# Balanced routing on one NeuronCore: each expert's list built inside its own round, and a token's state kept as one number in place of a one-hot row

## The chip, the core and the metric

The kernel runs on one core of a Trainium2 chip. The metric is device time in microseconds (us), from the timed runs of the whole program; a profiled execution, taken separately, shows what each engine does. The engines are TensorE (PE, with its weight loads listed as PEld), VectorE (DVE), ScalarE (ACT), GpSimd (POOL) and SyncE (SP, which here only issues DMAs).

## The reference, cut to what matters

Two blocks follow each other. The first is a gated linear attention with a state of 48 x 48 per head, over 4 sequences of 768 steps and 8 heads. Its output, as a matrix x of 3072 tokens by 384, goes into a layer of 8 experts with a fixed capacity:

```python
cap = N // E                                  # 3072 / 8 = 384 tokens for each expert
logits = x @ w_gate
order = np.argsort(-logits.flatten())         # all (token, expert) pairs, best first
for idx in order:
    tok, e = (int(idx) // E, int(idx) % E)
    if assigned[tok] >= 0 or counts[e] >= cap:
        continue
    assigned[tok] = e
    counts[e] += 1
for e in range(E):
    mask = assigned == e
    out[mask] = np.maximum(x[mask] @ w1[e], 0.0) @ w2[e]     # 384 -> 1024 -> 384
```

So every token gets one expert and every expert exactly 384 tokens. The greedy order matters only where an expert fills up: until then each token simply takes its best open expert.

## The kernel before, in words

**Attention** runs to about 170 us and ends with `logits`, a tile of 128 partitions by 24 columns by 8 experts: a token is one partition and one column. Alongside it, `begin` and its inner `part` prepare round 0: each token's best expert as a one-hot row `choice`, and `over`, how far its best logit lies above a lower bound.

**Rounds.** `assign_and_run` replaces the greedy loop by seven rounds and a rest. A round (loop at L825) closes one expert at least. It finds, for the tokens without an expert, their best open expert (`choices`, L521), then searches for the level at which the first expert has as many takers as places (`search`, L587), and assigns every token above that level (`assign`, L608). The level is found digit by digit, five digits of 15 steps each. For one digit DVE compares `over` with 15 steps for all 24 columns (`above`, 128 x 360), PE counts takers per step and expert (`cnt`), and DVE picks the digit. Round 0 uses `digit_alone` (L539), with 24 small count matmuls and one that spreads the digit (L550). Later rounds use `digit_beside` (L554), with three count matmuls (L560) and one that sums over partitions (L575). `close` (L654) then sets the state for the next round.

**State.** `assigned` is a one-hot row of 8 per token. `choices` reduces it to `taken`, 0 or 1, to leave assigned tokens out. `left` numbers the experts that have no list yet, from 1 to 8.

**Lists.** `expert_list` (L660) returns twelve steps that make the list of one filled expert. `members` picks the expert `m`, its one-hot row `sel`, and by a product with `assigned` (`mine`) and a reduction the tokens of it (`member`). `place` counts along the columns and lets PE sum over the partitions before (`before`, L682). `index` reads the expert's number into SP and issues the DMAs of its weights. `lines` turns a token's place into one of three blocks of 128 lines (`pl`, `b`, `line`), while POOL prepares `number` (L711 to L715). Six steps `in_line` (L719) compare lines with 1 to 128, four columns of 128 at a time, into a 0/1 matrix of 128 x 24 x 128. `used` strikes the expert off. `tokens` (L732) multiplies that matrix by the tokens' numbers in 24 matmuls (L735), turns the sums into token numbers, lets POOL gather the rows of x by indirect DMA (L745), and puts the expert's work in a queue.

**The order of the work** is written out by hand, for PE, DVE, ACT and POOL. Two queues hold what is not yet issued. `pe_work` holds the pieces of the experts' work: for an expert three turns (three transposes each, L772), 24 pieces of the first product (`up`, L783) and 24 of the second (`down`, L794), 51 pieces in all. `dve_work` holds the steps of a list. `some(queue, n)` issues the next n. A digit of `digit_beside` issues `slots[0]` pieces ahead of its L560 and `slots[1]` ahead of L575, and one and two list steps behind these. The slots are 2 and 1 in rounds 1 and 2, and 4 and 3 from round 3 on; the first digit of rounds 2 and 3 has 4 more. `assign` issues two pieces ahead of its matmul `sums` (L617) and eight behind. When a list is done and at least 12 pieces are queued, the last two of them are moved behind the new expert's turns.

The lists of rounds 0, 1 and 2 are made at once, in the round that fills the expert: in round 0 beside `idle_turns` (L811), matmuls without use that keep PE busy, in rounds 1 and 2 with a piece of `pe_work` behind each step. From round 3 on the list stays in `dve_work` and is made during the next round's search. After the last round the tokens left over take the last open expert and its list is made. With nothing else to come, the remaining pieces run to the end.

There is a second way through, `exact`, which runs only if the decays were out of range or the search did not end well. It is not run here.

The steps above act through a few helpers, so most DVE rows of the profile carry a helper's line: L396 is `tt` (two tensors), L400 `ts` (a tensor and one or two scalars), L403 `stt` (tensor, scalar, tensor), L406 `reduce`. A scalar is a constant or one value per partition.

Of the kernel before, what the change touches and what calls it, by code (L numbers as in the profile page):

```python
# [2 lines left out]

# [7 lines left out]
FP32 = mybir.dt.float32  # L11
# [13 lines left out]
def kernel(  # L25
# [313 lines left out]

    first = ramp(E, "first", -1, E + 1)  # L340
# [67 lines left out]

    places = rt([E], "places", FP32, 1)
# [4 lines left out]
    assigned = rt([NT, E], "assigned", BF16, 1)  # L414
# [52 lines left out]
    def begin():  # L467

        nc.vector.memset(places[:], float(CAP))
        nc.vector.memset(wanted[:], float(CAP))  # L470
        nc.vector.memset(penalty[:], 0.0)
        nc.vector.memset(full[:], 1.0)
        nc.vector.tensor_copy(out=left[:], in_=count[:, 0:E])
        nc.vector.memset(assigned[:], 0.0)
        nc.vector.memset(lowest[:], 0.0)
        choice, over = rt([NT, E], "choice", BF16), rt([NT], "over")

        def part(c0, c1):
            n = c1 - c0

            def of(t):
                return t[:].rearrange("p (b c) -> p b c", b=B)[:, :, c0:c1]

            def of_e(t):
                return t[:].rearrange("p (b c) e -> p b c e", b=B)[:, :, c0:c1]

            def over_e(t):
                return t.unsqueeze(3).to_broadcast((128, B, n, E))

            best, pick = rt([B, n], "best0"), rt([B, n], "pick0")  # L490
# [6 lines left out]
            reduce(pick[:], masked[:], ALU.max)  # L497
            tt(of_e(choice), masked[:], over_e(pick[:]), ALU.is_equal)

        return (choice, over), part  # L500

    def assign_and_run(begun=None, also=None, again=None, exact=None):
# [18 lines left out]
        def choices():  # L521
# [8 lines left out]
            reduce(pick[:], masked[:], ALU.max)  # L530

            taken = rt([NT], "taken")
            reduce(taken[:], assigned[:], ALU.max)
            stt(pick[:], taken[:], 100.0, pick[:], ALU.mult, ALU.add)
            choice = rt([NT, E], "choice", BF16)
            tt(choice[:], masked[:], col(pick[:], E), ALU.is_equal)
            return choice, best

        def digit_alone(above, choice, unit):  # L539

            r = bank("cnt", "r")
            for c in range(NT):
                nc.tensor.matmul(out=r[0:NTH, 0:E], lhsT=above[:, c, :], rhs=choice[:, c, :],
                                 start=(c == 0), stop=(c == NT - 1))
# [42 lines left out]
        def search(choice, over, digits, slots, first=0):  # L587

            digit = None
            for steps, unit, size in digits:  # L590
                above = rt([NT, NTH], "above", BF16)
                if digit is None:
                    tt(above[:], col(over[:], NTH), row(steps[:], NTH), ALU.is_ge)
                else:
                    stt(above[:], col(over[:], NTH), digit, row(steps[:], NTH), op, ALU.is_ge)
                    new = rt([NT], "over")
                    ts(new[:], over[:], digit, op)
                    over = new
                if slots:
                    digit, op = digit_beside(above, choice, size, (slots[0] + first, slots[1]))  # L600
                else:
                    digit, op = digit_alone(above, choice, unit)
                first = 0
            new = rt([NT], "over")
            ts(new[:], over[:], digit, op)
            return new

        def assign(choice, over, slots):  # L608
# [10 lines left out]
            tt(assigned[:], assigned[:], sure[:], ALU.add)  # L619
# [3 lines left out]
        def assign_exact(choice, over, slots):  # L623
# [17 lines left out]
            tt(assigned[:], assigned[:], sure[:], ALU.add)  # L641
# [10 lines left out]
            tt(assigned[:], assigned[:], tie[:], ALU.add)  # L652
# [7 lines left out]
        def expert_list():  # L660
# [3 lines left out]
            def members():  # L664
                score, m, sel = rt([E], "score"), rt([1], "m"), rt([E], "sel")
# [33 lines left out]
            def lines():  # L699
# [3 lines left out]
                tt(pl[:], L["incl"][:], L["r"][:, 0:1].to_broadcast((128, NT)), ALU.add)  # L703
                tt(pl[:], pl[:], L["member"][:], ALU.mult)
# [14 lines left out]
            def in_line(c0, c1):  # L719
                def go():  # L720
                    n = c1 - c0
                    tt(L["in_line"][:, c0:c1],
                       L["line"][:, c0:c1].unsqueeze(2).to_broadcast((128, n, 128)),
                       count[:].unsqueeze(1).to_broadcast((128, n, 128)), ALU.is_equal)
                return go

            def used():
                used = rt([E], "used")
                stt(used[:], left[:], 1.0, L["sel"][:], ALU.add, ALU.mult)
                tt(left[:], left[:], used[:], ALU.subtract)  # L730

            def tokens():  # L732
                r = bank("tokens", "r")
                for c in range(NT):
                    nc.tensor.matmul(out=r[:, 0:2 * TE], lhsT=L["in_line"][:, c, :],  # L735
                                     rhs=L["number"][:, c].rearrange("p a n -> p (a n)"),
                                     start=(c == 0), stop=(c == NT - 1))
                pair = rt([2, TE], "pair")
# [19 lines left out]
                in_line(c, c + PART) for c in range(0, NT, PART)] + [used, tokens]  # L758
# [59 lines left out]
        with tc.manual_schedule(engines=engines):  # L818
# [5 lines left out]
            beside_choices = {2: 4, 3: 4}  # L824
            for rnd in range(E - 1):  # L825
                slots, more = pace.get(rnd, (4, 3)), beside_choices.get(rnd, 0)
                if exact:
                    choice, best = choices()
# [9 lines left out]
                else:  # L838
                    if rnd == 0:
                        choice, over = begun  # L840
                    else:
                        choice, best = choices()
                        over = rt([NT], "over")
                        level_keys(best[:], over[:])
# [21 lines left out]
            while dve_work:  # L866
                some(dve_work, 1)
                some(pe_work, 1)
            choice, _ = choices()
            tt(assigned[:], assigned[:], choice[:], ALU.add)  # L870
# [148 lines left out]
```

## Time and profile before

| | us |
|---|---|
| median of three timed runs | 509.3 (509.28 to 511.03) |
| the profiled execution's own time | 511.35 |
| its span, first to last instruction | 509.6 |
| PE busy | 459.8 (90%) |
| DVE busy | 268.6 (53%) |
| ACT busy | 128.4 (25%) |
| POOL busy | 110.3 (22%) |
| mean granted PE clock | 0.964 |
| first piece of the first product (L783) starts | 201.0 |
| last PE instruction ends | 499.9 |

How to read it: busy time is that of executed instructions; a matmul's end is modelled and holds its drain, so rows of PE overlap a little. In a timeline a row gives the start, the duration (for several merged instructions, from the first start to the last end), the engine, line and operation, what is written from what, the shapes and a count; in brackets stands the idle time of the engine ahead of it and what ended that. The row PEclk shows the clock granted to PE in 40 slices of the span, in tenths.

### The profile page before, as it was taken

What the parts mean: (1) busy time and instruction counts of PE and PEld (TensorE: products, weight loads), DVE (VectorE), ACT (ScalarE), POOL (GpSimd) and SP (SyncE); (2) the same over time, 40 slices, a digit from 0 to 9 for tenths busy, and PEclk for the clock granted to TensorE, in tenths of its full rate; (3) what the DMA queues carried; (4) which work ended last, traced back from release to release, by engine and by line L of the source; (5) the groups of instructions that cost most, each with busy time, mean ns of one, the idle gap of its engine ahead of it and who ended that gap; (6) DMA issues with size and microseconds to landing.
All of it is one profiled execution on the core that took longest, in us unless ns stands there. A gap on an engine that the chain in (4) does not pass through costs nothing.

```text
span 509.6 us, 11773 instructions
## 1 busy us (share of the span) xinstructions
PE 459.8 (90%) x4848; PEld 304.0 (60%) x4848; DVE 268.6 (53%) x887; ACT 128.4 (25%) x301; POOL 110.3 (22%) x172
## 2 busy tenths in 40 slices
PE   2999999999999579898899998699899989999992
PEld 1778888887888435455466555355556555656551
DVE  6466666666677474766754568168666671000000
ACT  2455455544432001111111210121120210212210
POOL 2134333333231012013022003101303233002010
PEclk9999999999999659999999999599999999999997
DMA  9988997985211034053072007107243576000000
GB/s 158 187 167 178 192 201 165 188 172 123 66 34 50 17 130 165 1 207 117 17 251 74 16 13 283 47 6 258 78 163 124 184 237 239 32 0 33 14 17 35
DMA packets 118399, 59.11 MB, mean 116 GB/s; under 512 B 101664, under 2 KB 112960, under 8 KB 118336
## 3 DMA queue, kind: packets, MB, share of 16 engines
q1 hardware_dynamic: 111760, 44.06, 34.9%
q0 software_dynamic: 3072, 9.44, 5.7%
q10 hardware_dynamic: 3504, 4.77, 2.7%
q8 instruction: 40, 0.66, 0.6%
q14 instruction: 23, 0.19, 0.1%
HBM read 48.77 MB, written 9.49 MB: 114 GB/s over the span
## 4 chain that ended last, share of the span: by engine, by line
PE 63%; issue 17%; DVE 11%; POOL 4%; DMA 2%; ACT 1%; POOLq 0%; DVEq 0%
PE H L783 15%; PE O L794 14%; PE Y L247 5%; PE T L193 4%; PE A L230 4%; PE L L161 4%; PE L L165 3%; PE Y L257 2%; PE X L273 2%; PE dS L212 2%; DMA xe<-xd,token 2%; POOL out_dram L799 2%; PE X L287 2%; POOL xe L745 2%; DVE above L403 2%
## 5 line engine op out<-in xcount | busy, mean ns | idle before, releaser
L783 PE MATMUL H<-xeT,w 128*128 128x384 f32 x384 | 134.5, 499 | 1.7 <-ACT xeT L775 1.7
L794 PE MATMUL O<-w,hT 128*128 128x384 f32 x384 | 132.3, 492 | 0.5 <-issue 0.5
L783 PEld LDWEIGHTS H<-xeT,w 128*128 128x128 f32 x384 | 70.9, 193 | 52.8 <-issue 8.8
L794 PEld LDWEIGHTS O<-w,hT 128*128 128x128 f32 x384 | 70.1, 190 | 46.7 <-issue 5.6
L787 ACT ACTIVATE hT<-H 128x384 f32<-128x384 f32 x64 | 31.4, 491 | 114.2 <-PE H L783 111.2
L799 POOL DMA_INDIRECT out_dram<-o,token x24 | 24.3, 1014 | 143.7 <-ACT o L798 142.8
L235 DVE COPY_PREDICATED am<-mask,A 128x512 f32<-128x512 int32 x48 | 32.4, 727 | 29.0 <-PE A L230 29.0
L798 ACT COPY o<-O 128x384 f32<-128x384 f32 x24 | 11.5, 479 | 101.0 <-PE O L794 94.5
L396 DVE TENSOR_TENSOR in_line<-line,count 128x512 bf16<-128x512 f32 x48 | 31.6, 708 | 0.2
L745 POOL DMA_INDIRECT xe<-xd,token x24 | 24.1, 1004 | 34.1 <-DVE best L406 7.4
L185 POOL TENSOR_TENSOR kg<-k,ek 128x384 f32<-128x384 f32 x24 | 25.4, 1057 | 28.0 <-ACT ek L173 22.3
L161 PE MATMUL L<-g,wcum 128*128 128x384 f32 x48 | 23.0, 564 | 8.1 <-DVE count L329 8.1
L247 PE MATMUL Y<-v,am 128*64 128x48 f32 x768 | 28.0, 224 | 0.0
L247 PEld LDWEIGHTS Y<-v,am 128*64 128x64 f32 x768 | 24.7, 138 | 4.0 <-issue 3.7
L775 ACT COPY xeT<-Xe 128x384 f32<-128x384 f32 x24 | 10.6, 483 | 64.4 <-PE Xe L772 63.6
L230 PE MATMUL A<-qT,kT 48*64 48x128 f32 x768 | 26.7, 278 | 0.0
L711 POOL TENSOR_TENSOR past<-b,ramp_nt 128x48 f32<-128x48 f32 x8 | 2.2, 278 | 106.1 <-DVE b L396 106.1
L170 DVE TENSOR_SCALAR dl<-L 128x384 f32<-128x384 f32 x24 | 13.4, 557 | 21.1 <-PE L L165 21.1
L165 PEld LDWEIGHTS L<-ind,g 128*64 128x64 f32 x384 | 13.9, 144 | 14.1 <-issue 14.1
L396 DVE TENSOR_TENSOR own<-cnt,mine 120x64 f32<-120x64 f32 x30 | 6.7, 223 | 29.5 <-PE cnt L560 29.1
L230 PEld LDWEIGHTS A<-qT,kT 48*64 48x64 f32 x768 | 21.5, 137 | 0.2
L172 ACT ACTIVATE eq<-dl 128x384 f32<-128x384 f32 x24 | 12.6, 523 | 29.4 <-DVE dl L170 28.8
(170 smaller groups left out, 584.9 us busy)
## 6 DMA issues: line engine op xcount, KB each, us to landing
w<-in_moe_w_dram SPq DMA_DIRECT2D x16, 1536.0 KB, 8.6
f<-in_f_logit_dram SPq DMA_DIRECT2D x24, 192.0 KB, 4.7
q<-in_q_dram SPq DMA_DIRECT2D x24, 192.0 KB, 4.2
k<-in_k_dram SPq DMA_DIRECT2D x24, 192.0 KB, 4.6
v<-in_v_dram SPq DMA_DIRECT2D x24, 192.0 KB, 4.4
xd<-x ACTq DMA_DIRECT2D x24, 192.0 KB, 3.4
xe<-xd,token POOLq DMA_INDIRECT x24, 3.1
out_dram<-o,token POOLq DMA_INDIRECT x24, 2.6
```

Source lines behind the costliest of these rows:

```text
L161: nc.tensor.matmul(out=Lv, lhsT=wcum[:], rhs=g[:, :, 0:DH], start=True, stop=True)
L165: nc.tensor.matmul(out=ends[DP * r:DP * r + DP, :, hp], lhsT=g[:, 2 * hp + r, :], rhs=ind[:], start=True, stop=True)
L185: nc.gpsimd.tensor_tensor(out=kg[:, :, 0:DH], in0=G["k"][:], in1=ek[:], op=ALU.mult)
L230: nc.tensor.matmul(out=A[par][HC * j:HC * j + HC, 128 * hp:128 * hp + 128], lhsT=G["kT"][rows, hp, HC * j:HC * j + HC], rhs=G["qT"][rows, ...
L235: nc.vector.copy_predicated(am[:, par], mask[:].unsqueeze(1).to_broadcast((128, HP, 128)), A[par][:].rearrange("s (a t) -> s a t", t=128))
L247: nc.tensor.matmul(out=Y[par][HC * j:HC * j + HC, DH * hp:DH * hp + DH], lhsT=G["am"][:, par, hp, HC * j:HC * j + HC], rhs=G["v"][:, 2 * h ...
L396: nc.vector.tensor_tensor(out=out_, in0=a, in1=b, op=op)
L745: nc.gpsimd.indirect_dma_start(out=xe[:], out_offset=None, in_=xd[:, :], in_offset=bass.IndirectOffsetOnAxis(ap=token[:, i:i + 1], axis=0))
L783: nc.tensor.matmul(out=L["H"][:, 0:CAP], lhsT=L["w1"][:, d, 128 * ft:128 * ft + 128], rhs=xT[:, d, :], start=(d == 0), stop=(d == DC - 1))
L787: nc.scalar.activation(out=hT[:, ft, :], in_=L["H"][:, 0:CAP], func=AF.Relu)
L794: nc.tensor.matmul(out=L["O"][:, 0:D], lhsT=hT[:, ft, 128 * i:128 * i + 128], rhs=L["w2"][:, ft, :], start=(ft == 0), stop=(ft == FC - 1))
L799: nc.gpsimd.indirect_dma_start(out=outs[next(tiles)][:, :], out_offset=bass.IndirectOffsetOnAxis(ap=L["token"][:, i:i + 1], axis=0), in_=o ...
```

## The change

Four things change.

- **Every list at once.** The list is made in its own round in every round, with one piece of `pe_work` behind each of its twelve steps (in round 0 two idle turns behind each but the last two, so far three behind each). The slots from round 3 on become 3 and 2, the first digit of every round from 2 on gets 4 more, and `assign` has three pieces ahead of its matmul and seven behind. `used` goes behind `tokens`.
- **A number per token.** `taken` is no longer 0 or 1: it holds the number of the token's expert (8 for expert 0 down to 1), and 0 for a token without one. `assigned`, `mine` and `sel` go. `member` is one comparison of `taken` with `m`. `take` writes it, in two steps. `choices` keeps assigned tokens out by a large negative term in `over`. `left` runs from 8 to 1, so of several filled experts the lowest comes first, and the expert's number takes one more step.
- **Lines by column.** Each of the 24 columns is compared in an instruction of its own, with its line as the scalar, against a new bf16 tile `counts` of 1 to 128.
- **Round 0 in parts.** `above` is computed in three parts of eight columns, each ahead of the count matmuls that use it, and the step that brings `over` up to date goes behind the matmul that spreads the digit. The token sums of round 0's list are issued four columns at a time, behind their comparisons.

The diff, without the parts of the exact way:

```diff
@@ begin @@
-        nc.vector.tensor_copy(out=left[:], in_=count[:, 0:E])
-        nc.vector.memset(assigned[:], 0.0)
+        nc.vector.tensor_copy(out=left[:], in_=first[:])
+        nc.vector.memset(taken[:], 0.0)
...
-        def choices():
+        def picks():
...
-
-            taken = rt([NT], "taken")
-            reduce(taken[:], assigned[:], ALU.max)
-            stt(pick[:], taken[:], 100.0, pick[:], ALU.mult, ALU.add)
-            choice = rt([NT, E], "choice", BF16)
+            return best, pick, masked
+
+        def choices(best, pick, masked):
+
+            over, choice = rt([NT], "over"), rt([NT, E], "choice", BF16)
+            level_keys(best[:], over[:])
+            stt(over[:], taken[:], CLOSED / 16, over[:], ALU.mult, ALU.add)
             tt(choice[:], masked[:], col(pick[:], E), ALU.is_equal)
-            return choice, best
-
-        def digit_alone(above, choice, unit):
+            return choice, over
...
+        def take(over, pick, op=ALU.is_ge):
+            new = rt([NT], "new")
+            stt(new[:], over, 0.0, pick[:], op, ALU.mult)
+            tt(taken[:], taken[:], new[:], ALU.add)
+
+        def reached(above, over, digit, op, steps, c0, c1):
+
+            n = c1 - c0
+            over = over[:, c0:c1].unsqueeze(2).to_broadcast((128, n, NTH))
+            steps = steps[:].unsqueeze(1).to_broadcast((128, n, NTH))
+            if digit is None:
+                tt(above[:, c0:c1], over, steps, ALU.is_ge)
+            else:
+                stt(above[:, c0:c1], over, digit, steps, op, ALU.is_ge)
+
+        def digit_alone(above, parts, choice, unit):
 
             r = bank("cnt", "r")
             for c in range(NT):
+                if c % 8 == 0:
+                    parts(c, c + 8)
                 nc.tensor.matmul(out=r[0:NTH, 0:E], lhsT=above[:, c, :], rhs=choice[:, c, :],
                                  start=(c == 0), stop=(c == NT - 1))
...
@@ search, round 0 @@
-                    digit, op = digit_alone(above, choice, unit)
+                    new, op_new = digit_alone(above, parts, choice, unit)
+                    over = less(over, digit, op)
+                    digit, op = new, op_new
...
@@ assign @@
-            tt(assigned[:], assigned[:], sure[:], ALU.add)
+            take(over[:], pick)
...
@@ expert_list: members @@
-                ts(sel[:], left[:], m[:], ALU.is_equal)
-                mine = rt([NT, E], "mine", BF16)
-                tt(mine[:], assigned[:], row(sel[:], E), ALU.mult)
                 member = rt([NT], "member")
-                reduce(member[:], mine[:], ALU.max)
-                L.update(member=member, m=m, sel=sel)
+                ts(member[:], taken[:], m[:], ALU.is_equal)
+                L.update(member=member, m=m)
...
@@ index @@
-                ts(e[:], L["m"][:], -1.0, ALU.add, 0.0, ALU.max)
+                ts(e[:], L["m"][:], -1.0, ALU.mult, float(E), ALU.add)
+                ts(e[:], e[:], E - 1, ALU.min)
...
@@ lines @@
-                tt(pl[:], L["incl"][:], L["r"][:, 0:1].to_broadcast((128, NT)), ALU.add)
-                tt(pl[:], pl[:], L["member"][:], ALU.mult)
+                stt(pl[:], L["incl"][:], L["r"][:, 0:1], L["member"][:], ALU.add, ALU.mult)
...
@@ in_line @@
-                    n = c1 - c0
-                    tt(L["in_line"][:, c0:c1],
-                       L["line"][:, c0:c1].unsqueeze(2).to_broadcast((128, n, 128)),
-                       count[:].unsqueeze(1).to_broadcast((128, n, 128)), ALU.is_equal)
+                    for c in range(c0, c1):
+                        ts(L["in_line"][:, c], counts[:], L["line"][:, c:c + 1], ALU.is_equal)
+                    if alone:
+                        token_sums(c0, c1)
...
-                in_line(c, c + PART) for c in range(0, NT, PART)] + [used, tokens]
+                in_line(c, c + PART) for c in range(0, NT, PART)] + [tokens, used]
...
@@ the rounds @@
-            beside_choices = {2: 4, 3: 4}
             for rnd in range(E - 1):
-                slots, more = pace.get(rnd, (4, 3)), beside_choices.get(rnd, 0)
+                slots, more = pace.get(rnd, (3, 2)), 4 if rnd > 1 else 0
...
-                some(dve_work, len(dve_work))
-                (assign_exact if exact else assign)(choice, over, (2, 8))
-                dve_work.extend(expert_list())
+                (assign_exact if exact else assign)(choice, over, pick, (3, 7))
+                dve_work.extend(expert_list(rnd == 0))
+                while dve_work:
+                    some(dve_work, 1)
+                    if rnd:
+                        some(pe_work, 1)
+                    elif len(dve_work) > 1:
+                        idle_turns(2)
                 if rnd == 0:
-                    while dve_work:
-                        some(dve_work, 1)
-                        idle_turns(3)
                     idle_turns(27)
...
-                if rnd in (1, 2):
-                    while dve_work:
-                        some(dve_work, 1)
-                        some(pe_work, 1)
                 close()
...
-            choice, _ = choices()
-            tt(assigned[:], assigned[:], choice[:], ALU.add)
+            best, pick, masked = picks()
+            unassigned = rt([NT], "unassigned")
+            ts(unassigned[:], taken[:], -1.0, ALU.mult)
+            take(unassigned[:], pick)
```

More of the change, by code (lines that the diff above doesn't have):

```diff
@@ L413 @@
     left = rt([E], "left", FP32, 1)
[L414 removed]
+    taken = rt([NT], "taken", FP32, 1)
     lowest = rt([E], "lowest", FP32, 1)
@@ L496, in part @@
                first[:].unsqueeze(1).unsqueeze(1).to_broadcast((128, B, n, E)), ALU.mult)
-            reduce(pick[:], masked[:], ALU.max)
-            tt(of_e(choice), masked[:], over_e(pick[:]), ALU.is_equal)
-        return (choice, over), part
+            reduce(of(pick), masked[:], ALU.max)
+            tt(of_e(choice), masked[:], over_e(of(pick)), ALU.is_equal)
+        return (choice, over, pick), part
     def assign_and_run(begun=None, also=None, again=None, exact=None):
@@ L618, in assign, with assign_exact, take_all @@
             some(pe_work, slots[1])
-            tt(assigned[:], assigned[:], sure[:], ALU.add)
+            take(over[:], pick)
             tt(places[:], places[:], r[:, 0:E], ALU.subtract)
             ts(full[:], places[:], 0.5, ALU.is_lt)
-        def assign_exact(choice, over, slots):
+        def assign_exact(choice, over, pick, slots):
+            def take_all(mask):
+                some_ = rt([NT], "some")
+                reduce(some_[:], mask[:], ALU.max)
+                take(some_[:], pick, ALU.is_gt)
             after, notfirst, _ = exact
@@ L728, in used, with token_sums, tokens @@
                 used = rt([E], "used")
-                stt(used[:], left[:], 1.0, L["sel"][:], ALU.add, ALU.mult)
+                ts(used[:], left[:], L["m"][:], ALU.is_equal)
+                stt(used[:], left[:], 1.0, used[:], ALU.add, ALU.mult)
                 tt(left[:], left[:], used[:], ALU.subtract)
[L732 to L735, printed above, removed]
+            def token_sums(c0, c1):
+                if c0 == 0:
+                    L["sums"] = bank("tokens", "r")
+                for c in range(c0, c1):
+                    nc.tensor.matmul(out=L["sums"][:, 0:2 * TE], lhsT=L["in_line"][:, c, :],
                                      rhs=L["number"][:, c].rearrange("p a n -> p (a n)"),
                                      start=(c == 0), stop=(c == NT - 1))
+            def tokens():
+                if not alone:
+                    token_sums(0, NT)
+                r = L["sums"]
                 pair = rt([2, TE], "pair")
```

62 lines of the change are left out of this document (34 added, 28 removed).

## The prediction

> **What bounds the kernel now.** I read the page first, for the shape of the span, then busy time by stage, then the timeline of TensorE (PE) and VectorE (DVE) from the first choice to the last list, then who waited for whom.
>
> ```profile
> span 509.6 us, 11773 instructions
> ...
> PEclk9999999999999659999999999599999999999997
> ```
> ```profile
> 181.50:192.40 10.90, 9.48 (x61) 4.98 (x61) 7.33 (x25) 0.00 (x0) 1.30 (x3) 0.63 0.55 200
> 316.50:332.50 16.00, 10.13 (x51) 5.77 (x51) 4.70 (x21) 2.42 (x5) 3.76 (x4) 0.68 0.16 50
> ```
>
> A slice of the page is 12.7 us. The clock row drops twice after the attention part: in slices 14 and 15 (round 0) and in slice 26. The windows say the same (columns: stage, length, busy time of PE, its weight loads, DVE, ACT, POOL, then granted clock, DMA share, GB/s): from 316.5 to 332.5 the granted clock is 0.68 and PE is busy for 10.13 of 16 us. PE is the bound from 201 us on, since the experts' products are all there is left to do; what can be won there is only time in which PE stands still or runs at a low clock. These are the places:
>
> ```profile
> 316.51 0.21 PE L575 MATMUL cnt<-parts,ones 120*128 120x120 bf16 x1 [0.95 <-DVE parts L396]
> 316.57 0.75 PE L735 MATMUL tokens<-number,in_line 128*128 128x6 bf16 x24
> 321.12 0.90 PE L772 MATMUL Xe<-ident,xe 128*128 128x128 f32 x3 [3.81 <-DMA xe<-xd,token]
> ...
> 325.07 1.65 PE L783 MATMUL H<-xeT,w 128*128 128x384 f32 x2 [0.57 <-ACT xeT L775]
> ...
> 326.78 3.50 PE L783 MATMUL H<-xeT,w 128*128 128x384 f32 x6
> ...
> 332.49 0.17 PE L617 MATMUL sums<-count,ones 128*128 128x8 bf16 x1 [0.80 <-DVE count L406]
> ```
> ```profile
> 361.94 0.49 PE L772 MATMUL Xe<-ident,xe 128*128 128x128 f32 x3
> 362.27 0.22 PE L575 MATMUL cnt<-parts,ones 120*128 120x120 bf16 x1
> ...
> 365.34 8.01 PE L783 MATMUL H<-xeT,w 128*128 128x384 f32 x24 [0.54 <-ACT xeT L775]
> ```
> ```profile
> 415.57 0.16 PE L682 MATMUL before<-total,ltri 128*128 128x1 bf16 x1 [1.52 <-DVE e L400]
> ```
> ```profile
> PE sums L617 <- DVE count L406: 5.3, 6, 1.2
> ```
>
> What PE's queued work costs when nothing stops it:
>
> ```profile
> 223.80 0.17 PE L682 MATMUL before<-total,ltri 128*128 128x1 bf16 x1
> 223.83 6.70 PE L794 MATMUL O<-w,hT 128*128 128x384 f32 x20
> 230.36 0.75 PE L735 MATMUL tokens<-number,in_line 128*128 128x6 bf16 x24
> ```
>
> A product is two matmuls. 20 of them fill 223.83 to 230.36, so a queued product (a "piece") costs 0.653 us, and a "turn" of three transposes 0.33 (361.94 to 362.27). An expert is 3 turns and 48 products, 51 pieces. In round 4 the queue of pieces is empty when the tokens of the next expert are still being found: its list, put off into that round's search, has twelve steps, handed out three to a digit, so that the tokens come with the fourth.
>
> **The change, rounds 1 to 7.** The pieces are the same before and after, so I count only stalls. First those that go.
>
> (1) Round 4. From 316.5 to 332.5 PE has the token sums (0.75), nine transposes (1.0), six pieces (3.9: the rows with x2 and x6, and the two behind the last L575) and small things (0.2): 5.85 of 16 us. The six pieces show the low clock too, at 0.58 a matmul (3.50 by 6). Leave out the 0.8 at the end (next point but one), add the 0.95 ahead of 316.51, and 10.3 us are lost. In the new order a round hands out 5 digits of 3+2 pieces, 4 more in its first, 3+7 in the assignment and 12 beside its own list: 51, one expert. The queue, counted through: 49 pieces after round 0; round 1 takes 15 + 10 + 10 up to its tokens, which add 51, and 2 behind them: 63; round 2 the same with 4 more: 73; and then each round takes 29 + 10 + 10, which leaves 24 at the tokens, and ends at 73 again. Two of the 24 are set behind the turns, and so 22 pieces, 14.4 us, stand before the first transpose, which needs 4.6 (316.57 to 321.12). The stall goes, and the low clock with it. (2) Round 5: 361.94 to 365.34 is 3.4 us, with 1.1 of work: 2.3 go, for the same reason. (3) The `sums` matmul waits 0.8 us in five of these rounds (six waits of 5.3 in all, less round 0's 1.2). Three pieces before it in place of two fill 0.653 of that: 3.3 in all. (4) The last list: `before` waits 1.52. PE gets one piece more ahead of it (0.65), and DVE's chain from the tokens to `total` loses the wide steps `taken`, `choice`, `assigned`, `mine` and `member` and gains the narrow ones of `used`, `close` and `take`: some 0.6 shorter by their rows' sizes, between 0 and 0.9. I take 1.2 as gone. Sum: 17.1.
>
> Now what comes late instead. A digit needs time on DVE between its two matmuls:
>
> ```profile
> 212.42 0.21 PE L575 MATMUL cnt<-parts,ones 120*128 120x120 bf16 x1 [0.21 <-DVE parts L396]
> ...
> 214.22 0.35 PE L560 MATMUL cnt<-choice,above 128*120 128x64 bf16 x3 [0.24 <-DVE above L403]
> ...
> 215.51 0.21 PE L575 MATMUL cnt<-parts,ones 120*128 120x120 bf16 x1 [0.21 <-DVE parts L396]
> ```
>
> 1.80 us must pass from one digit's L575 to the next L560, and 1.29 from there to L575. Three pieces are 1.96, two are 1.31: PE hides both, barely, and a digit of rounds 3 to 6 becomes PE's 3.5 us. When turns fall into a digit (fourth digit of each round by my count), one piece and two turns are 1.31 against 1.80, one turn and one piece 0.98 against 1.29: 0.6 lost, four times, 2.4. Rounds 1 and 2 keep their 2+1 and lose what they lost. Net of rounds 1 to 7: 17.1 - 2.4 = 14.7 us.
>
> All this asks that the list itself stays hidden, now in every round:
>
> ```profile
> 224.04 0.18 DVE L396 TENSOR_TENSOR pl<-mincl,before 128x24 f32<-128x24 f32 x1 [3.64 <-PE before L682]
> ...
> 225.14 3.96 DVE L396 TENSOR_TENSOR in_line<-line,count 128x512 bf16<-128x512 f32 x6
> ```
> ```profile
> 141.65 0.25 DVE L400 TENSOR_SCALAR unit<-ones,step 128x128 bf16<-128x128 bf16 x1
> 141.81 0.23 DVE L400 TENSOR_SCALAR steps<-count,step 128x15 f32<-128x15 f32 x1
> 141.95 0.25 DVE L400 TENSOR_SCALAR unit<-ones,step 128x128 bf16<-128x128 bf16 x1
> ```
>
> `used` moves behind `tokens`, so 9 pieces, 5.88 us, lie between `before` and the tokens (10 so far). DVE needs 5.3 (223.80 to 229.10) so far. The new comparison is one instruction a column. Its nearest row is `unit`: same operation, 128 bf16 elements, a scalar per partition. It lasts 0.25, and the next starts 0.16 after it. 24 x 0.16 + 0.09 = 3.93: nothing is won on DVE, nothing lost, and with one step of `lines` less (0.21) the list needs 5.1, with 0.8 to spare. From below, a column costs the 0.14 of the step on 15 elements (141.81 to 141.95), 3.4 in all, a gain that PE's pieces would hide; from above there is no overlap at all, 24 x 0.246 = 5.9 (a rival). I take 0.16, the row of the same size. The Trainium skill says, in "VectorE: DVE Perf Modes", section "The DRAIN you can't avoid", that after every operation the pipe empties before the next starts, which speaks against cutting six instructions into 24. The trace does not agree for independent ones, by these rows; by the page's rule the time would be that rival's.
>
> **Round 0**, where PE has only idle turns to fill with.
>
> ```profile
> 172.22 0.60 DVE L403 SCALAR_TENSOR_TENSOR above<-over,cnt,steps 128x360 bf16<-128x360 f32 x1 [0.25 <-PE cnt L550]
> 172.73 0.24 DVE L400 TENSOR_SCALAR over<-over,cnt 128x24 f32<-128x24 f32 x1
> ...
> 172.87 0.75 PE L543 MATMUL cnt<-choice,above 128*15 128x8 bf16 x24 [0.69 <-DVE above L403]
> ```
> ```profile
> 181.59 1.12 PE L815 MATMUL nothing<-idle,ones 128*128 128x384 bf16 x3
> ...
> 182.83 0.36 DVE L396 TENSOR_TENSOR mine<-assigned,sel 128x192 bf16<-128x192 bf16 x1
> ...
> 183.61 0.21 DVE L677 TENSOR_TENSOR_SCAN mincl<-onesc,member 128x24 f32<-128x24 f32 x1
> ...
> 184.06 0.16 PE L682 MATMUL before<-total,ltri 128*128 128x1 bf16 x1 [1.36 <-DVE e L400]
> ...
> 184.98 0.28 POOL L711 TENSOR_TENSOR past<-b,ramp_nt 128x48 f32<-128x48 f32 x1 [26.13 <-DVE b L396]
> ...
> 185.75 0.62 POOL L715 TENSOR_TENSOR number<-past 128x144 bf16<-128x144 f32 x1
> ...
> 191.62 0.75 PE L735 MATMUL tokens<-number,in_line 128*128 128x6 bf16 x24
> ```
> ```profile
> DMA to landing us min/median/max: 3.0/3.1/5.2
> ```
>
> A digit: a third of `above` costs about 0.34 (between 0.24 for 24 elements and 0.60 for 360) and lets the next start after 0.25, so the thirds end at 0.34, 0.59 and 0.84; eight matmuls (0.25) behind the last end at 1.14 where all 24 now end at 1.40. 0.26 in four digits; the first waits for `choice` and wins nothing. The `over` step moves between `filled` and the next `above` and takes the gap there (0.24 in 0.25): I take 0.9. `sel` becomes `member`, `mine` and the old `member` go: 183.61 - 182.83 = 0.78. The two steps of `take` replace one under the wait for `sums`: 0, at most 0.2. `before` comes 1.7 earlier, at 182.4. Then PE sets the pace: 6 idle turns of 0.32 (1.12 for three, less the last one's drain; the clock is low here), then six groups of four token matmuls (0.13) with two idle turns (0.64) between: 5.9 us, sums done at 188.3; now they end at 192.37. DVE's columns are done at 187.4, so PE ends last. 4.1 us earlier. The second scalar step for the expert's number costs the weights' issue 0.1 and nothing behind it. One thing can take some back: the gathers now start while the first weights are still flying; a gather lands in 3.0 to 5.2, so up to 2.2 is lost. I take 4.0, bounds 1.8 and 4.7.
>
> **The sum.** 14.7 + 4.0 = 18.7 us. The profiled execution took 511.35 (span 509.6 and 1.75 around it), so it would take 492.65; the median of the runs is 2.05 below it, so 490.6.
>
> **The rivals.** A, the list is uncovered by GpSimd. DVE and POOL hinder each other here:
>
> ```profile
> 157.70 0.78 DVE L396 TENSOR_TENSOR masked<-logits,best 128x160 f32<-128x160 f32 x1
> ...
> 158.80 0.31 DVE L396 TENSOR_TENSOR masked<-masked,first 128x160 f32<-128x160 f32 x1
> ```
> ```profile
> 413.90 0.40 DVE L400 TENSOR_SCALAR sel<-left,m 128x8 f32<-128x8 f32 x1
> ```
>
> The same size takes 0.78 in place of 0.31, and a scalar step on 8 elements 0.40, where `over` with 24 takes 0.24. POOL's three steps for `number` (184.98 to 186.37, 1.4 us) run beside the columns and are needed for the tokens. If they only get through when the columns are done, the list needs 5.1 + 1.4 = 6.5, 0.6 more than PE covers, in seven lists, and round 0 gives up about 1: 495.8. For it: 24 short steps stand where six long ones stood, and each can meet POOL. Against: POOL has 5 us to find gaps. The Trainium skill, "SBUF — State Buffer", section "Who interferes with whom", has a lock: a scalar step in a two-port mode and a GpSimd instruction block each other for a whole instruction; no row here shows that kind beside POOL's steps.
>
> B, columns without overlap: 5.9 + 1.2 = 7.1 a list, 1.2 uncovered, seven times, and 2 in round 0: 501.0. The rows of `unit` speak against it.
>
> C, slower than before: columns that each collide. A list takes 24c + 1.2, uncovered beyond 5.88, seven times. The 18.7 us are used up at c = 0.31. At the 0.40 of `sel` a list is 10.8, 4.9 uncovered, 34.4 us, and 4 in round 0: 529. Against it: only one in many rows collides so.
>
> D, the stalls of rounds 4 and 5 are not a matter of the list's place and stay: 12.6 us less won, 503.2. The count of pieces speaks against.
>
> **How the numbers follow.** Forecast 0.67, A 0.15, B 0.06, D 0.05, C 0.04; 0.03 for a gain above all bounds. The forecast's own range is 487 to 493: round 0 may give 2.2 less or 0.7 more, the turns may fall where they cost none of the 2.4, and the last list may lose its 0.3 too. The range 486 to 499 takes in A and the better half of B. Half a per cent, 2.5 us, is about what a measurement of this kernel can tell from no change; only C is slower, and little lies between: 0.94, 0.02, 0.04.
>
> **What would show it.** Right: no second drop in the clock row; `tokens` of round 0 ends near 188.3, the first H near 197; `tokens` waits for nothing in rounds 1 to 7; a digit of rounds 3 to 6 lasts 3.5 us; last PE work near 481. Wrong: columns over 0.2 us apart, `number` later than 5 us after `before`, or PE waiting at L735 or for xe.

## The result and the profile after

The changed kernel takes 495.81 us (median of four runs, 495.5 to 498.6), the kernel before 509.29 beside it: a ratio of 0.974 [0.970, 0.978], 13.5 us won. The forecast was 490.6, 5.2 us too low. The time lies outside the forecast's own range of 487 to 493; it is held only by the stated range of 486 to 499, which was made wide enough for rival A. The profiled execution took 495.5, with a span of 493.7. Four runs that took 536 us or more, where the others of the same kernel took under 518, are left out of the medians below.

The page of the kernel after, span and clock row:

```profile
span 493.7 us, 11897 instructions
...
PEclk9999999999999859999999999999999999999998
```

The drop of slice 26 is gone, that of slices 14 and 15 (round 0) is still there. The windows of the kernel after (columns as in the prediction): from `pair`, which copies the token sums, to the first transposes; from there to the first piece; from there to the last PE work:

```profile
187.20:194.90 7.70, 4.72 (x30) 2.64 (x28) 4.23 (x19) 0.00 (x0) 3.11 (x3) 1.00 0.97 359
194.90:199.46 4.56, 3.99 (x17) 2.47 (x18) 0.00 (x0) 1.43 (x3) 0.00 (x0) 0.63 0.01 4
199.46:483.90 284.44, 276.96 (x1134) 161.61 (x1134) 142.36 (x655) 51.55 (x108) 52.28 (x65) 1.00 0.31 109
```

The same three stretches of the kernel before:

```profile
192.40:197.40 5.00, 4.86 (x30) 2.72 (x28) 4.21 (x17) 0.00 (x0) 2.99 (x3) 1.00 0.76 247
197.40:201.00 3.60, 2.94 (x17) 1.65 (x17) 0.00 (x0) 1.44 (x3) 0.37 (x1) 1.00 0.30 94
201.00:499.90 298.90, 280.11 (x1134) 163.77 (x1134) 143.53 (x536) 51.55 (x108) 52.57 (x65) 0.98 0.30 104
```

The last rows are rounds 1 to 7: 298.9 became 284.4, 14.5 us won. PE stands still for 7.5 us (284.44 less 276.96) in place of 18.8, which is 11.3; the other 3.1 are the same work (x1134) at a clock of 1.00 in place of 0.98. The first two rows are round 0's way from the token sums to the first piece, and it became longer: 12.26 us in place of 8.60. Much of the gain that is missing went there. In the timeline of the kernel after:

```profile
169.04 0.28 DVE L399 TENSOR_TENSOR above<-over,steps 128x120 bf16<-128x120 f32 x1
...
181.62 0.16 PE L718 MATMUL before<-total,ltri 128*128 128x1 bf16 x1 [0.90 <-DVE e L403]
...
182.78 4.17 DVE L403 TENSOR_SCALAR in_line<-counts,line 128x128 bf16<-128x128 bf16 x24
...
182.91 0.39 SPq L729 DMA_DIRECT2D w<-in_moe_w_dram  x1
183.20 0.45 POOL L751 TENSOR_TENSOR number<-past 128x144 bf16<-128x144 f32 x1
...
183.70 0.24 PE L773 MATMUL tokens<-number,in_line 128*128 128x6 bf16 x4
...
187.22 0.16 DVE L403 TENSOR_SCALAR pair<-tokens 128x6 f32<-128x6 f32 x1 [0.27 <-PE tokens L773]
...
188.62 1.21 POOL L788 DMA_INDIRECT xe<-xd,token  x1 [4.97 <-DVE masked L399]
...
194.90 0.55 PE L815 MATMUL Xe<-ident,xe 128*128 128x128 f32 x3 [2.98 <-DMA xe<-xd,token]
```

The same points of the kernel before:

```profile
170.00 0.53 DVE L396 TENSOR_TENSOR above<-over,steps 128x360 bf16<-128x360 f32 x1
...
185.16 0.39 SPq L692 DMA_DIRECT2D w<-in_moe_w_dram  x1
...
192.40 0.17 DVE L400 TENSOR_SCALAR pair<-tokens 128x6 f32<-128x6 f32 x1 [2.80 <-PE tokens L735]
...
193.80 1.34 POOL L745 DMA_INDIRECT xe<-xd,token  x1 [7.43 <-DVE best L406]
```

The first `above` starts 0.96 us earlier. That is the attention part, which the change doesn't touch. Counted from `above`, `pair` comes after 18.18 us in place of 22.40, 4.2 earlier; the first piece, at 199.46 and 201.01, comes after 30.42 in place of 31.01, only 0.6 earlier. Between the two, the first gather takes 6.28 us to its transposes (3.61 before), and from there to the first piece 4.56 (3.60 before), at a granted clock of 0.63.

### The profile page after: what moved, and what is told of

The parts are those of the page before. It is cut to its first block, busy times and chain, and to the rows that moved or that the text cites. A ratio compares the mean times of both kernels' runs of the same rounds, so it can differ in the third digit from the quotient of the medians.

```text
span 493.7 us, 11897 instructions
## 1 busy us (share of the span) xinstructions
PE 454.5 (92%) x4832; PEld 301.1 (61%) x4832; DVE 267.9 (54%) x1034; ACT 128.4 (26%) x301; POOL 109.7 (22%) x172
## 4 chain that ended last, share of the span: by engine, by line
PE 64%; issue 18%; DVE 9%; POOL 4%; DMA 1%; POOLq 0%; ACT 0%; DVEq 0%
PE O L837 15%; PE H L826 15%; PE Y L248 5%; PE T L194 4%; PE A L231 4%; PE L L162 3%; PE Y L258 3%; PE L L166 2%; PE X L274 2%; PE dS L213 2%; POOL out_dram L842 2%; DVE above L406 2%; PE X L288 2%; PE cnt L590 1%; PE nothing L858 1%
## 5 line engine op out<-in xcount | busy, mean ns | idle before, releaser
L826 PE MATMUL H<-xeT,w 128*128 128x384 f32 x384 | 131.8, 493 | 0.6 <-ACT xeT L818 0.6
L403 DVE TENSOR_SCALAR in_line<-counts,line 128x128 bf16<-128x128 bf16 x192 | 33.7, 254 | 0.3
L180 POOL TENSOR_TENSOR gl<-spans 128x4 f32<-128x4 f32 x20 | 4.0, 199 | 66.3 <-DVE logits L290 51.9
```

The source lines that it names most:

```text
L403: nc.vector.tensor_scalar(out=out_, in0=a, scalar1=s1, scalar2=s2, op0=op0, **kw)
L826: nc.tensor.matmul(out=L["H"][:, 0:CAP], lhsT=L["w1"][:, d, 128 * ft:128 * ft + 128], rhs=xT[:, d, :], start=(d == 0), stop=(d == DC - 1))
```

## The experiments

For round 0 the theory was that the gathers queue behind the 3 MB of expert 0's weights, and that PE's wait for them costs clock as well. The rival: gathers are slow here for a reason of POOL or of their own, and moving the weights changes nothing. For rounds 1 to 7 the question was which edit won the 14.5 us. Times are medians, and a ratio is to the kernel before on the same chip. That kernel took 512.5 and 512.1 us on the two chips of most experiments and 509.3 on the first one, so a ratio there should not be set beside the 0.974; what is compared is the stretches of the profiles. The attention part ends at another moment in each execution (the first count of round 0 starts between 169.1 and 171.3), so profiles are compared by two stretches: from that first count to the first piece (30.09 us in the kernel after), and from there to PE's last work (284.4).

### The second half of the weights goes behind the gathers

```diff
+                if not alone:
+                    second()
...
+                if alone:
+                    nc.sync.dma_start(out=L["w2"][0:1, 0, 0:1], in_=L["xe"][TE - 1][0:1, 0:1])
+                    L["second"]()
```

`second` issues the DMA of `w2`. In round 0 (`alone`) it goes behind the gathers, and a transfer of four bytes makes SP wait for the third of them first.

> The changed kernel, but round 0 issues its expert's second weight array only when its three gathers have landed. Theory (the gathers of round 0 wait behind the 3 MB of weights that are still flying): the gathers land in about 3 us, the first transpose comes 3.6 after the first gather's start in place of 6.3, PE keeps its clock, the first product starts near 196 in place of 199.5, and the whole takes 492 to 493. Rival (GpSimd is held up by DVE's short steps while it makes the gathers' descriptors): nothing changes, 495.8.

It took 492.82 us, a ratio of 0.961 [0.957, 0.965]. Its timeline:

```profile
189.43 1.21 POOL L792 DMA_INDIRECT xe<-xd,token  x1 [5.16 <-DVE wanted L406]
...
192.81 0.55 PE L822 MATMUL Xe<-ident,xe 128*128 128x128 f32 x3
...
196.40 0.91 PE L833 MATMUL H<-xeT,w 128*128 128x384 f32 x2 [0.57 <-ACT xeT L825]
```

From the gather to the transposes 3.38 us, from there to the first piece 3.59, and PE waits for no xe (the rows that a gather brings). The first piece comes 26.4 us after the first count, 3.7 earlier than in the kernel after. The later rounds take 284.4 again: nobody misses the late half. The theory holds: round 0's list did come 4 us earlier, and the weights took it back.

How they did so is seen in the DMA view, by queue (q1 carries the weights, q0 the gathers; packets, MB, share of the 16 engines). The kernel after, from 191 to 192 us, from 192.5 to 193 and from 193 to 193.5:

```profile
q1 hardware_dynamic: 243, 0.37, 106.3%
```
```profile
q0 software_dynamic: 26, 0.12, 62.3%
q1 hardware_dynamic: 67, 0.08, 50.0%
```
```profile
q0 software_dynamic: 55, 0.18, 97.3%
q1 hardware_dynamic: 14, 0.02, 10.6%
```

And this experiment, from 191 to 191.5, the first half microsecond with a gather's packet in it:

```profile
q0 software_dynamic: 9, 0.04, 44.0%
```

With the second array out of the way, the first packet of a gather moves 1.6 to 2.1 us after its start (189.43 to 191.0–191.5). In the kernel after that would be at 190.7 at the latest, but no packet of a gather moves until 192.5, while the weights fill the engines. Only as the weights run out, with 67 packets in the next half microsecond in place of some 120, do the gathers get through.

### More idle turns, so that PE does not stand still

```diff
-                    idle_turns(27)
+                    idle_turns(47)
```

> The changed kernel with 47 idle turns ahead of round 0's transposes in place of 27, so that PE is busy until the late gathers land. Theory (of the 3.6 us lost behind the tokens, 2.7 are the gathers' and 0.9 the low clock that follows PE's 3 us of waiting): first transpose as late as before relative to the first gather (6.3), but the first product 3.6 behind it in place of 4.6, 29.2 from the first count. Rival (the clock falls whatever PE does there): 30.1.

One run, 496.42 us. Its windows from the end of the sums to the transposes, and from there to the first piece:

```profile
189.70:197.47 7.77, 7.77 (x49) 4.72 (x48) 4.19 (x19) 0.00 (x0) 3.11 (x3) 1.00 0.90 326
197.47:200.50 3.03, 2.46 (x20) 1.76 (x17) 0.00 (x0) 1.44 (x3) 0.00 (x0) 1.00 0.00 1
```

PE no longer stands still and its clock stays at 1.00: the second stretch is 3.03 us in place of 4.56. The first is as long as without the edit. The sums themselves came 0.5 later here, so the first piece comes 29.16 us after the first count, 0.9 earlier. Of the 3.6 us that round 0 gave back in the profiled execution, some 0.9 to 1.5 are the clock's, the rest is the wait for the transfer.

### The thirds taken back

```diff
-                if c % 8 == 0:
-                    parts(c, c + 8)
+                if c == 0:
+                    parts(0, NT)
```

> Round 0's comparison of the expert numbers is one instruction again, as in the kernel before; all else as in the changed kernel. If the thirds let the 24 matmuls of the first digit start while the rest is still compared, the first digit takes 2.03 us again in place of 1.90, four digits together 0.5 us more, and the first H comes 30.6 us after the first count in place of 30.1. If the thirds only make more instructions, the digit stays at 1.9. Rounds 1 to 7 as in the changed kernel, 284.4 us within 1 us, so the whole would be between 495 and 497 us.

`above` compares `over` with the 15 steps of a digit. The second and third digit of round 0 in this experiment:

```profile
171.94 0.60 DVE L406 SCALAR_TENSOR_TENSOR above<-over,cnt,steps 128x360 bf16<-128x360 f32 x1 [0.25 <-PE cnt L580]
...
173.97 0.60 DVE L406 SCALAR_TENSOR_TENSOR above<-over,cnt,steps 128x360 bf16<-128x360 f32 x1
```

And in the kernel after:

```profile
171.08 0.87 DVE L406 SCALAR_TENSOR_TENSOR above<-over,cnt,steps 128x120 bf16<-128x120 f32 x3 [0.25 <-PE cnt L580]
...
172.98 0.87 DVE L406 SCALAR_TENSOR_TENSOR above<-over,cnt,steps 128x120 bf16<-128x120 f32 x3
```

A digit lasts 2.03 us again in place of 1.90. From the first `above` to `before` are 13.31 us in place of 12.58: the thirds win 0.7, of which four digits make 0.5 and the first one 0.2. The rest of the expectation missed: one run took 499.37, and the first piece came 31.6 us after the first count, not 30.6. Its clock stayed low for longer after the wait for the gathers: it was 0.50 until 206, where the kernel after had 1.00 from 200 on, and the first two matmuls of the first product took 1.65 in place of 0.91. The two runs with the lists put off and with lines by four, which have the thirds, show the same 1.65 and a clock of 0.50 until 204 and 205. How long the low clock lasts behind such a wait thus differs between executions, and the kernel after was profiled in one where it was short. A single time does not show 0.7 us; the rows do.

### The lists put off again from round 3 on

The slots go back to 4 and 3, and `assign` again has two pieces ahead of its matmul `sums` and eight behind. All else stays as in the changed kernel.

```diff
-                slots, more = pace.get(rnd, (3, 2)), 4 if rnd > 1 else 0
+                slots, more = pace.get(rnd, (4, 3)), {2: 4, 3: 4}.get(rnd, 0)
...
-                while dve_work:
+                while dve_work and rnd < 3:
```

> The changed kernel, but from round 3 on with the old order: slots 4 and 3, lists made during the next round's search, two pieces ahead of sums. Theory (what was won from round 1 on is PE's stalls, by the order of the pieces alone): the stall ahead of round 4's gathers and the low clock come back, the stretch from the first product to the last goes from 284.4 back to about 297, the whole takes 507 to 509. Rival (the narrower state and the column comparisons make the rounds shorter by themselves): about 500.

It took 510.21 us, a ratio of 0.994 [0.991, 0.998]. The stall of round 4 is back in its timeline:

```profile
317.65 0.75 PE L773 MATMUL tokens<-number,in_line 128*128 128x6 bf16 x24
322.38 0.90 PE L815 MATMUL Xe<-ident,xe 128*128 128x128 f32 x3 [3.97 <-DMA xe<-xd,token]
```

The later rounds take 299.7 us, as long as before the change (298.9), although the number per token and the columns are still there; some 1.4 of it is likely the low clock behind round 0's wait, since the next run has that too. So the whole gain of rounds 1 to 7 comes from the first of the four changes, the place of the lists together with the number of pieces at each point. This run does not part the two, except that `sums` waits 5.3 us again in place of 2.2: so 3.1 of the 14.5 belong to the third piece ahead of it.

### Lines by four columns again

```diff
-                        ts(L["in_line"][:, c], counts[:], L["line"][:, c:c + 1], ALU.is_equal)
+                    tt(L["in_line"][:, c0:c1],
+                       L["line"][:, c0:c1].unsqueeze(2).to_broadcast((128, n, 128)),
+                       count[:].unsqueeze(1).to_broadcast((128, n, 128)), ALU.is_equal)
```

> The changed kernel, but with the old comparison of four columns in one instruction. Theory (a column alone takes as long as a quarter of four, and PE's nine pieces cover either): within 0.5 us of the changed kernel, 495.3 to 496.3. Rival (the column comparison is part of the gain): 498 or more.

It took 496.48 us, a ratio of 0.967 [0.963, 0.971], 0.2 us above what was expected and well below the rival's 498. Its later rounds take 285.8 in place of 284.4, but they begin at a clock of 0.50 that lasts until 205. No difference is left that the columns would have to explain. Six instructions last 3.95 us in its list, 24 columns 4.17 in the list quoted above.

### Every column compared twice

```diff
-                    for c in range(c0, c1):
+                    for c in [c for c in range(c0, c1) for _ in range(2)]:
```

> The changed kernel with every column comparison done twice, so that a list's columns take 8.35 us in place of 4.17. Theory (PE's nine pieces cover 5.88 us of a list, and what is beyond that is paid in full): tokens waits 3.6 us in each of seven lists, and round 0 is 2 to 4 longer: 522 to 526. Rival (other work takes up the wait, or DVE's time is never seen): under 505.

It took 560.58 us, a ratio of 1.094 [1.089, 1.099], far above the 522 to 526 that were expected. The list of round 1 in its timeline:

```profile
225.40 0.17 PE L718 MATMUL before<-total,ltri 128*128 128x1 bf16 x1
...
226.59 11.23 DVE L403 TENSOR_SCALAR in_line<-counts,line 128x128 bf16<-128x128 bf16 x48
...
237.88 0.19 PE L773 MATMUL tokens<-number,in_line 128*128 128x6 bf16 x1 [0.27 <-DVE in_line L403]
```

48 columns take 11.23 us, not the 8.3 of 0.174 each: the second write of a column does not overlap the first. In the middle of the list it starts 0.28 us after the first, which lasts 0.25, and the next column starts 0.17 after that. So the last token sums end 12.7 us after `before`; PE's nine pieces cover 5.9 of it and the sums alone would take 0.75, which leaves 6.0 uncovered. The windows' row from the first piece to the end:

```profile
203.25:546.70 343.45, 309.96 (x1134) 177.96 (x1134) 185.65 (x823) 51.55 (x108) 51.84 (x65) 0.92 0.26 90
```

The later rounds take 59 us more than the 284.4. Seven lists uncovered by 6.0 are 42 of them; the clock was 0.92 on the way in place of 1.00, which the expectation had left out. The numbers fit lists paid in full and a rest that goes to the clock, but the two were not measured apart.

### Round 2 with the wide slots

```diff
-            pace = {0: None, 1: (2, 1), 2: (2, 1)}
+            pace = {0: None, 1: (2, 1)}
```

> The changed kernel, but round 2 too takes 3 and 2 pieces a digit. Theory (only PE's stalls count, and a digit with 2 and 1 leaves PE 0.9 us idle): five digits give 4.0 to 4.6 us, 14 pieces are still left at each list's tokens, 9 us of cover against the 7 that the last gather needs, so nothing new stalls: about 491.5. Rival (the queue gets too short and the transposes wait for the gathers): 494 to 497.

It took 492.47 us, a ratio of 0.960 [0.956, 0.964]; the later rounds take 280.6, 3.8 less. Two digits of round 2 in the kernel after:

```profile
242.61 0.35 PE L590 MATMUL cnt<-choice,above 128*120 128x64 bf16 x3 [0.24 <-DVE above L406]
...
243.90 0.21 PE L605 MATMUL cnt<-parts,ones 120*128 120x120 bf16 x1 [0.21 <-DVE parts L399]
...
245.70 0.35 PE L590 MATMUL cnt<-choice,above 128*120 128x64 bf16 x3 [0.24 <-DVE above L406]
```

With three pieces a digit is DVE's 3.09 us, and in this experiment, with five:

```profile
241.55 0.30 PE L590 MATMUL cnt<-choice,above 128*120 128x64 bf16 x3
...
243.06 0.22 PE L605 MATMUL cnt<-parts,ones 120*128 120x120 bf16 x1
...
245.11 0.30 PE L590 MATMUL cnt<-choice,above 128*120 128x64 bf16 x3
```

3.56 us, no wait, and two pieces (1.31) more done: 0.84 won a digit, 4.2 in five, of which 3.8 arrived at the end.

### Both: the weights and round 2

> The changed kernel with the second weight array late in round 0 and 3 and 2 pieces in round 2. Theory (the two stalls lie one after the other and add up): 26.4 us from the first count to the first product and 280.6 from there to the last, 488.5 to 489.5. Rival (with the products 3 us earlier something else is late, the second weights or round 1's list): 491 or more.

It took 489.24 us, a ratio of 0.953 [0.950, 0.956]: faster than both kernels. The first piece comes 26.17 us after the first count and the later rounds take 280.56, so the two gains add up.

### The kernel before once more

> The kernel before once more, for a second profile of it. Theory (its profiled execution happened to be one of the longer ones, by how the attention part's start and the clock after the gathers fell out): the stretch from round 0's first count matmul to the first product is 30.4 again and from there to the last product 298.8, both within 1 us, and what differs in the span lies ahead of round 0. Rival (the two long stretches themselves vary by some us): either differs by 2 or more.

It took 512.45 us, a ratio of 1.001 [0.998, 1.004]. Its profile differs from the first one of the same kernel by 1.5 us in the end of the attention part, 0.5 in the first stretch and 2.1 in the second (300.9 in place of 298.8). The expectation of 1 us for each stretch was too tight: 2 us between two single profiles prove nothing. The stall of round 4 and its clock of 0.7 stand in both. And its PE waits 0.74 us for xe in round 0, where the gathers started at 191.77 and the weights filled the engines until 193.5: the kernel before already stood at the edge.

## Why the prediction was right, and where it was off

**Rounds 1 to 7: 14.7 forecast, 14.5 measured.** The stalls of rounds 4 and 5 went with the place of the lists, as counted; the waits view of the kernel after has no row for xe in these rounds. `sums` waited 4.1 us there and now waits 1.0, so 3.1 went in place of 3.3. The last list's `before` waited 1.52 and now waits 0.17, so 1.35 went in place of 1.2:

```profile
PE sums L651 <- DVE count L409: 2.2, 7, 1.3
```
```profile
407.39 0.16 PE L718 MATMUL before<-total,ltri 128*128 128x1 bf16 x1 [0.17 <-DVE e L403]
```

(Of the 2.2 us, 1.3 are round 0's.) The digits with turns cost about what was forecast, 0.5 us a round in place of 0.6: in round 3 two digits, 274.16 to 280.80, hold seven pieces and three turns, 6.1 us of work with the counts, and last 6.6. The full digits are PE's 3.5:

```profile
267.04 0.30 PE L590 MATMUL cnt<-choice,above 128*120 128x64 bf16 x3
...
270.60 0.30 PE L590 MATMUL cnt<-choice,above 128*120 128x64 bf16 x3
```

So the terms of the sum that can be read singly are borne out. That the total came within 0.2 us is luck: beside the second profile of the kernel before, with its 300.9, the same gain is 16.5.

**Round 0: 4.0 forecast, 0.6 measured.** That is below even the lower bound of 1.8. The sums came 4.2 earlier where 4.1 was forecast, but by errors that cancel: `before` came 1.5 earlier in place of 1.7 (the thirds win 0.13 in each of four digits and not 0.26), and the sums behind it 2.7 in place of 2.4. The step that failed is the one behind them: "a gather lands in 3.0 to 5.2, so up to 2.2 is lost. I take 4.0". The loss was taken from the slowest gather seen, not from the time at which the weights are through. That could have been worked out. The weights are issued in `index`, near `before`, so they moved by only 2.25 us in all (185.16 to 182.91) and the gathers by 5.18 (193.80 to 188.62). The weights filled the engines until about 195.0 before, hence until some 192.8 after, and gathers started at 188.62 would meet them. The measured loss is 2.7 for the transfer and 0.9 for the clock, 3.6 in all; the clock's part had no term, and in three other runs the low clock lasted longer. One of the prediction's own signs of being wrong came with it: PE waited 2.98 us for xe. The first H came at 199.5 and the last PE work ended at 483.9, not near 197 and 481, while the other signs of being right did appear.

The Trainium skill, "DMA: Bandwidth & Descriptors", section "Queues, rings and completion order", says that each DMA engine goes round the queues that hold work for it, a packet from each. By that rule gathers that were in their queue by 190.7 should have moved beside the weights from then on. The rows by queue do not show that: 243 packets of the weights and none of a gather from 191 to 192. What makes the gathers come last stays open; only the order was seen.

**The conversion to the median: 2.4 of the 5.2.** The offset of 2.05 between the profiled execution before and its median was carried over as if it were the kernel's. It was no property of the kernel: after, the profiled one took 0.3 less than the median. Nor did 509.3, from three runs, settle the median: on two other chips, with 16 and 17 runs, the kernel before took 512.5 and 512.1, and single runs lay between 510.1 and 517.3. The account of the middle: 490.6, plus 0.2 to 0.3 (rounds), 3.4 (round 0) and 2.4 (offset), less 0.96 (attention) is 495.7.

**The rivals.** A gave 495.8, the time that was measured, but its mechanism did not occur: POOL's `number` is done at 183.65, 2.0 us after `before` and before the first sums at 183.70, and no token sums of a later round wait for anything. A number that fits does not prove a cause, and that the range held the time is luck too: it was widened for a rival that did not come, and what did come, gathers behind the weights, was worth more than the prediction allowed for. B and C did not occur: 24 columns take 4.17 us, 0.174 each, while one lasts 0.25. Only one of the 24 lasted 0.42; it started at 183.28, just behind POOL's `number`. The Trainium skill, "VectorE: DVE Perf Modes", lets the pipe empty after every operation (section "The DRAIN you can't avoid"), but lets an operation start earlier where nothing holds it (section "Two Vector instructions with no wait between them"); the columns agree with the second, and a second write of the same column, 0.28 behind a first of 0.25, with the first. D is refuted by the lists put off again.

## What to carry to other kernels

When a change makes a small transfer start earlier, look at what the DMA engines carry at its new time: it may land when the large transfer issued ahead of it ends, and no sooner. Work that is needed first should be issued first; here the late half of the large transfer cost nothing. Compare two profiles stretch by stretch from a common event, since a start that moves by a microsecond looks like a gain; and where PE can stand still, add the clock that it loses to the wait. Changes that go in together should be taken back one at a time before the gain is given to one of them.

## What the runs showed of the hardware

- Gathers issued behind 3 MB of weights moved no packet for at least 3.9 us (188.62 to 192.5), until the weights began to run out; with half of the weights issued behind them, the first packet came 1.6 to 2.1 us after the start.
- Behind a wait of 2.98 us on PE the granted clock was 0.63 over the next 4.56 us; with idle matmuls in the place of the wait it stayed at 1.00. Behind waits of 2.7 to 3.0 us in three other runs it was still 0.50 at 203 us, 6 us or more after the wait.
- Column comparisons into different columns start 0.174 us apart and last 0.25; with every column written twice the second write starts 0.28 after the first, and the mean is 0.234.
